# A linear-attention and token-mixing kernel: one load for w_phi, plain loads for the last weight rows, and kv blocks moved by matmuls

## The chip, the cores and the metric

One core of one Trainium2 chip. The metric is the device time of one execution in microseconds (us); smaller is better. The engines are TensorE (PE in the profile, with its weight loads as PEld), VectorE (DVE), ScalarE (ACT), GpSimd (POOL) and SyncE (SP). SP and ACT also issue the DMA transfers; each of the two has a DMA queue, and both queues run on the same 16 DMA engines. SBUF is the on-chip memory of 128 partitions, PSUM the accumulators that TensorE writes.

## The reference

`x` is 2048 tokens of 448 values, all in bf16. `xn` is its layer norm. Two branches read `xn`, and the output is `x + A(xn) + B(xn)`.

```python
# A: linear attention, 16 heads of 28
q, k, v = heads(xn @ wqkv)
pq, pk  = q @ w_phi[h], k @ w_phi[h]                    # a 28x28 matrix for each head
phi_q   = concat(softmax(pq), softmax(-pq))             # 56 features
phi_k   = concat(softmax(pk), softmax(-pk))
kv, z   = phi_k.T @ v, sum over tokens of phi_k
A       = concat_heads((phi_q @ kv) / (phi_q @ z + 1e-6)) @ wo
# B: a mixer
h  = gelu(layernorm(xn) @ w1)
hs = concat(h0 by +1 token, h1 by -1, h2 by +2, h3 by -2) @ w2
x1 = xn + hs
B  = x1 + gelu(layernorm(x1) @ w3) @ w4
```

## The kernel before

The tokens lie in 16 tiles of 128. Everything stays in SBUF between the steps; only `x`, the weights and the output cross to the chip's memory.

**Head.** `x` is loaded on SP's queue (tiles 0, 1, 2-3, then three transfers of four tiles). `wk` and `wq`, the key and query columns of `wqkv`, are loaded on ACT's queue and `wv` on SP's. The 448 rows of such a weight do not fill four blocks of 128 partitions, so `load_dup` (line 460) loads rows 0 to 383 in one transfer and then rows 384 to 447 *twice*, into both halves of the fourth block, by one transfer whose source reads the same 64 rows two times. TensorE transposes `wk` and `wq` (`trw`, line 653), and `fold` (line 674) multiplies them with `bd`, a matrix with the 28x28 blocks of `w_phi` on its diagonal, so that `xn @ wpk` gives `pk` at once. `bd` is zeroed by VectorE and filled by four DMAs on ACT's queue (line 503). VectorE and GpSimd make the layer norm: statistics and the scaling on VectorE, the power -1/2 on GpSimd (`ln_pow`, line 574). The first four tiles of `xn` are transposed by TensorE, the other twelve by DMA transposes on SP.

**K, V, Q.** For each pair of tiles, TensorE makes V (14 matmuls of 448 columns), K (14) and half of a Q group (14 of 512); ScalarE takes the exponentials of K and Q out of PSUM, ScalarE or VectorE copies V; VectorE sums the exponentials and GpSimd normalises (`phik<-phik,ksum`). W1 (`w,xnT`) follows, and after its last exponential ScalarE loads the gelu table (`warm2`, line 773) and takes the gelus of W1 (`gel`, `hq<-ps,fs`), which SP transposes one tile at a time by DMA into `hT`.

**The kv step.** 4 times 32 matmuls (`kv0` to `kv3`) sum `phi_k.T @ [v, 1]` over all tokens in one PSUM bank, two heads side by side in each of 8 column blocks. `kvc` (line 809) copies the bank to `kvs`. The wanted 28-row blocks stand on the partitions of `phi_k`; the numerator needs them on others, in `kvq`, with zeros around. Eight DMAs from SBUF to SBUF move them (line 819), seven of them issued by ACT and one by SP. `num` (line 888) waits for all of these.

**Mixer and end.** W2 (`w,hT`) reads `hT` of the tiles on both sides; VectorE adds `xn`, makes the second layer norm, and SP transposes it by DMA into `gT` (`gD`). H (`gT,w`) is the 448 to 1792 layer, followed by F (`w,phik` and `wo,xnT`), which sums both branches. Sixteen numerators (`kvq,eq`) are spread over this part.

Nothing here is in a hand-written order. The program is a list of tasks with a rank, dependencies and an assumed length; the class `Planner` (line 223) simulates the engines and fixes each engine's order, and for some tasks which of two engines takes them. `TI` and `TL` (line 448) are the assumed issue time and the assumed further delay of a DMA transpose. Each engine then runs its list strictly in order. `Recorder` derives the semaphore waits. All elementwise instructions are recorded from one line (L209), all activations from L205, all matmuls from L197, all plain DMAs from L212, the DMA transposes from L215. The names of tiles tell them apart; where memory is shared, a tile carries the name of its region (`wk`, `wq` and their transposes are `eq`, the gelu output and `wpq` are `hq`, the scaled `x1` is `wv`, numerator scratch is `vaug`, `h3` is `phik`, and attention outputs are `xnT`).

Of the kernel before, what the change touches and what calls it, by code (L numbers as in the profile page):

```python
# [5 lines left out]
ACT = mybir.ActivationFunctionType  # L6
ALU = mybir.AluOpType
# [338 lines left out]
def bass_parallel_sum__linear_kernel_hedgehog__mixer_s_mlp__prompt_kernel(  # L346
# [16 lines left out]
    with es:  # L363
# [53 lines left out]
        w4 = new("w4", FC * D).rearrange("p (c d) -> p c d", c=FC)  # L417
        gT = new("gT", 2 * 4 * 512).rearrange("p (b t c n) -> p b t c n", b=2, t=4, c=4)
        g_tok = view(wv_r, 4 * 512).rearrange("p (b t d) -> p b t d", b=2, t=2)
        kvs = new("kvs", 8 * 2 * HE).rearrange("p (c u n) -> p c u n", c=NC, u=2)  # L420
        kvq = new("kvq", 8 * 2 * HE).rearrange("p (c s n) -> p c s n", c=NC, s=2)
        ident = new("ident", 128)
        stat = {}
        for nm in ("st", "mv", "rs", "fs", "st2", "mv2", "rs2"):
            stat[nm] = new(nm, NT * 8, F32).rearrange("p (t c) -> p t c", t=NT)
        ksum = new("ksum", 8 * 32, F32).rearrange("p (b c) -> p b c", b=8)
        mhalf = new("mhalf", 8, F32)
        tiny = new("tiny", 2, F32)

        h3T = view(phik_r, 2 * FC * 512).rearrange("p (b c f) -> p b c f", b=2, c=FC)  # L430
# [14 lines left out]
        xs = carve(2 * D, F32).rearrange("p (b d) -> p b d", b=2)  # L445

        dve, pool = "DVE", "POOL"
        TI, TL = 1290, 1250
        P = Planner({"ps": 4, "h": 8, "g": 2, "gT": 2, "h3": 2, "o": 2, "oT": 2, "q": 2, "xs": 2, "ob": 4, "ks": 8})
        P.PATIENCE = {"PE": 60, "DVE": 80, "ACT": 80, "POOL": 80, "SP": 200}  # L450

# [7 lines left out]

        def load_dup(name, dst, src, rank, eng, cols=None, after=()):  # L460
            s = src if cols is None else src[:, cols]
            t = s[384:D, :]
            kb = 64 * (dst.ap[-1][1] * 2) / 1024
            twice = bass.AP(t.tensor, t.offset, [[0, 2]] + [list(a) for a in t.ap])
            return [load(name + "0", dst[:, 0:3, :], s[0:384, :].rearrange("(c p) d -> p c d", p=128), rank, eng, 6 * kb, after),
                    load(name + "1", dst[:, 3, :], twice, rank + 0.1, eng, 2 * kb, after)]

        def load(name, dst, src, rank, eng="SP", kb=100.0, after=()):
            return P.add(name, eng if isinstance(eng, dict) else {eng: 510}, None, rank, after,
# [28 lines left out]
        def memset(name, eng, ap, val, busy, rank):  # L498
            return P.add(name, eng, busy, rank, [], lambda t: R.ew(eng, "memset", ap, val))

        z_bd = memset("z_bd", dve, bd[0:CR, :], 0.0, 240, -20)
        phi4 = A_w_phi.rearrange("(c j) e f -> j e c f", j=4)
        l_bd = [P.add("bd%d" % j, "ACT", 690, -18.5 + j * 0.1, [z_bd],
                      lambda t, j=j: R.dma(bd[DH * j:DH * j + DH, :].rearrange("p (c f) -> p c f", c=NC)
                                           [:, :, DH * j:DH * j + DH], phi4[j], "ACT"), lag=1900) for j in range(4)]
        more_x(4, 4, -16)
        more_x(8, 4, -15)
        more_x(12, 4, -13)
# [7 lines left out]
                 [ident], [ident])  # L516

        t_id = P.add("ident", pool, 550, -19, [], ident_emit)
        t_mh = memset("mhalf", pool, mhalf[:, :], -0.5, 60, -18)
        z_h2 = memset("z_h2", pool, h_tok[:, 4:8, :, CR:128], 0.0, 330, 30)  # L520
        z_hT = memset("z_hTa", pool, hT[:, :, HALO - 2:HALO], 0.0, 60, 30)
# [127 lines left out]
        for t_, (w_sb, ld, rk) in enumerate(((wk, l_wk, -2), (wq, l_wq, -1))):  # L649
            nm = "kq"[t_]  # L650
            k = ("ps", "wT" + nm)

            def trw(t, w_sb=w_sb, k=k):
                for c in range(NC):
                    v = bank(P.slot[k], c // 2).bitcast(BF16)
                    for m in range(4):
                        R.tr(v[0:CR, 512 * (c % 2) + 128 * m:512 * (c % 2) + 128 * m + 128],
                             w_sb[:, m, CR * c:CR * c + CR], ident[:, :])
            tw = P.add("wT" + nm, "PE", 16 * (100 if t_ == 0 else 56), rk, ld + [t_id], trw, [k], mode=128)
            ev = []  # L660
            for d in range(2):
                def cp(t, k=k, d=d, t_=t_):
                    v = bank(P.slot[k], d).bitcast(BF16)[0:CR, :].rearrange("p (c n) -> p c n", c=2)
                    o = wT[0:CR, t_, 2 * d:2 * d + 2, :]
                    if t.eng == "ACT":
                        R.act(o, v, ACT.Copy)
                    else:
                        R.ew(dve, "tensor_copy", o, v)
                ev.append(P.add("wTc%s%d" % (nm, d), {"ACT": 905, "DVE": 620}, None, rk, [tw], cp, [k], lag=120))
            fold_done[nm] = []  # L670
            for mp in range(2):
                k2 = ("ps", "fold%s%d" % (nm, mp))

                def fold(t, k2=k2, mp=mp, t_=t_):
                    for d in range(2):
                        m = 2 * mp + d
                        for c in range(NC):
                            R.mm(bank(P.slot[k2], d)[:, CR * c:CR * c + CR], wT[0:CR, t_, c, 128 * m:128 * m + 128],
                                 bd[0:CR, CR * c:CR * c + CR], True, True)
                tf = P.add("fold%s%d" % (nm, mp), "PE", 8 * 49, rk + 2 + 5 * t_ + mp, ev + l_bd, fold, [k2], mode=128)  # L680

                def cpf(t, k2=k2, mp=mp, t_=t_):
                    v = both(P.slot[k2])[:, :, 0:D]
                    if t_ == 0:
                        o = wpk[:, 2 * mp:2 * mp + 2, :]
                    else:
                        o = wpq[:, 2 * mp:2 * mp + 2, :, :].rearrange("p b c (u d) -> p b (c u) d", u=2)[:, :, :, 0:56]
                        v = v.rearrange("p b (n d) -> p b n d", d=56)
                    if t.eng == "ACT":
                        R.act(o, v, ACT.Copy)  # L690
                    else:
                        R.ew(dve, "tensor_copy", o, v)
                fold_done[nm].append(P.add("foldc%s%d" % (nm, mp), {"ACT": 800, "DVE": 1010}, None, rk + 2 + 5 * t_ + mp,
                                           [tf] + ([z_wpq] if t_ else []), cpf, [k2]))
# [25 lines left out]
        for j in range(8):  # L720
# [15 lines left out]
            for i in (i0, i1):  # L736
                def red(t, i=i):
                    R.ew(dve, "tensor_reduce", ksum[:, P.slot[("ks", i)], :],
                         phik[:, i, 0:2 * D].rearrange("p (h e) -> p h e", e=DH), axis=AX.X, op=ALU.add)
                r1 = P.add("red%d" % i, dve, 1000, rk, ex, red, [("ks", i)], lag=110)  # L740

                def rec(t, i=i):
                    b = P.slot[("ks", i)]
                    R.ew(dve, "reciprocal", ksum[:, b, :], ksum[:, b, :])
                r2 = P.add("rec%d" % i, dve, 270, rk - 1, [r1], rec, [("ks", i)], lag=100)

                def nrm(t, i=i):
                    ph = phik[:, i, 0:2 * D].rearrange("p (h e) -> p h e", e=DH)
                    R.ew(t.eng, "tensor_tensor", ph, ph,
                         ksum[:, P.slot[("ks", i)], :].unsqueeze(2).to_broadcast([128, 2 * H, DH]), op=ALU.mult)  # L750
                k_ready[i] = P.add("nrm%d" % i, {"POOL": 1660, "DVE": 1000} if i in NRM_DVE else {"POOL": 1660}, None, rk, [r2], nrm, [("ks", i)])

        q_ready = {}
        for n in range(8):
# [52 lines left out]
                               + kv_pe[-1:], kv, [KV], mode=128))  # L807

        def kvc(t):
            R.ew(dve, "tensor_copy", kvs.rearrange("p c u n -> p (c u n)"), bank(P.slot[KV], 0)[:, 0:16 * HE])  # L810
        t_kvs = P.add("kvc", dve, 580, 100, [kv_pe[-1]], kvc, [KV])
        kv_dma = []
        for r in range(2):
            for s in range(2):
                for u in range(2):
                    def mvb(t, r=r, s=s, u=u):
                        p0, q0 = 56 * r + 28 * s, 64 * u + 28 * r
                        R.dma(kvq[q0:q0 + 28, :, s, HE * r:HE * r + DH + 1], kvs[p0:p0 + 28, :, u, HE * r:HE * r + DH + 1], t.eng)
                    kv_dma.append(P.add("kvd%d%d%d" % (r, s, u), {"SP": 850, "ACT": 560}, None, 125, [t_kvs, z_kvq], mvb, lag=2200))


        x1_ready, g_ready = {}, {}
# [3 lines left out]
        for j in range(8):  # L826
# [43 lines left out]
            def gd(t, j=j):  # L870
                R.dmaT(gT[:, P.slot[("gT", j // 2)], 2 * (j % 2):2 * (j % 2) + 2, :, :].rearrange("p t c n -> p (t c) n"),
                       g_tok[:, P.slot[("g", j)], :, :].rearrange("p t d -> p (t d)"))
            g_ready[i0] = g_ready[i1] = P.add("gD%d" % j, "SP", TI, G_RANK[j], ga, gd, gk, lag=TL)

        l_w3 = load_w("w3", w3, B_w3, 90, "SP", after=[xT_ready[15]])
        l_wo = load_dup("wo", wo, A_wo, 92, "SP", None, [xT_ready[15]])
# [6 lines left out]
        for i in range(NT):  # L883
# [4 lines left out]
            def num(t, i=i, g=g, jj=jj, k=k):  # L888
                bx, by = bank(P.slot[k], 0), bank(P.slot[k], 1)
                for s in range(2):  # L890
                    for c in range(NC):
                        at_ = 240 * s + 60 * c
                        for u, b in ((0, bx), (1, by)):
                            p = slice(64 * u, 64 * u + 56)
                            R.mm(b[:, at_:at_ + 60], eq[p, g, c, s, 128 * jj:128 * jj + 128], kvq[p, c, s, :], True, True)
            tn = P.add("num%d" % i, "PE", 8 * 28.5, NUM_RANK[i], q_ready[g] + kv_dma, num, [k] + ring, mode=64)

            def part(k, s):
# [51 lines left out]
            def od(t, i=i, g=g):  # L950
                R.dmaT(oT[:, P.slot[("oT", g)], i % 4 - 1:i % 4 + 1, :, :].rearrange("p t c n -> p (t c) n"),
                       o_tok[:, P.slot[("o", i // 2)], :, :].rearrange("p t d -> p (t d)"))
            oT_ready[i - 1] = oT_ready[i] = [P.add("oD%d" % (i // 2), "SP", TI, rk, [du], od, ok, lag=TL)]


        h3_ready = {}
# [97 lines left out]
```

## Time and profile before

| | us |
|---|---|
| median of 3 runs | 194.18 (193.66 to 195.72) |
| the profiled execution | 195.62 |
| its span in the profile | 193.7 |
| PE busy | 173.8 (90%) |
| DVE busy | 113.5 (59%) |
| ACT busy | 80.2 (41%) |
| POOL busy | 80.2 (41%) |

The profiled execution is 1.9 us longer than its span and 1.4 us above the median. Busy time on its own does not tell what an engine waits for: VectorE's 59% is an average over a stretch in which it is full and others in which it idles. A clock below 1.00 in the windows means that TensorE ran slower there. In the chain of waits, `ACTq` is ACT's instruction queue issuing a DMA, and `DMA` the time until a transfer's completion is seen.

### The profile page before, as it was taken

Reading aid. Unit: us, or ns where it says so; the run is one execution under the profiler, and the core shown is the slowest. Engines: PE = TensorE matmul, PEld = TensorE weight load, DVE = VectorE, ACT = ScalarE, POOL = GpSimd, SP = SyncE. Lnnn points to the kernel's source line nnn. Section 1 sums busy time; section 2 is a strip of 40 time slices with the busy share of each in tenths; the row PEclk is TensorE's granted clock in tenths of the full one; section 3 lists DMA queues with packets and bytes.
Section 4 is the critical chain, followed back from the end, with each engine's and each line's share of the span. In section 5 each row is a group of like instructions: output and inputs, shape, how many; then the busy total and the mean of one; then the engine's idle time right before and its main releaser. Section 6 shows DMA issues by size and latency. Waiting matters only on the chain.

```text
span 193.7 us, 4832 instructions
## 1 busy us (share of the span) xinstructions
PE 173.8 (90%) x2062; PEld 110.9 (57%) x2062; DVE 113.5 (59%) x298; ACT 80.2 (41%) x97; POOL 80.2 (41%) x121
## 2 busy tenths in 40 slices
PE   0228999999999959958999999999999999999994
PEld 0217555577666524424555666666666666666693
DVE  3614999978493255996999544292461677120222
ACT  0226889999997044203345213252042455200000
POOL 4501788999962010611343462052340642240440
PEclk9999999999999996997999999999999999999999
DMA  6984054669902626567109516027120122210111
GB/s 172 275 254 118 31 97 99 81 156 390 302 20 54 89 46 123 58 128 143 33 0 109 111 48 57 3 67 143 51 54 3 47 58 54 58 47 3 47 54 47
DMA packets 43864, 18.07 MB, mean 93 GB/s; under 512 B 34690, under 2 KB 43330, under 8 KB 43842
## 3 DMA queue, kind: packets, MB, share of 16 engines
q1 hardware_dynamic: 41108, 16.65, 38.5%
q10 hardware_dynamic: 2734, 1.10, 2.2%
q8 instruction: 16, 0.26, 0.6%
q14 instruction: 6, 0.05, 0.1%
HBM read 8.00 MB, written 1.84 MB: 51 GB/s over the span
## 4 chain that ended last, share of the span: by engine, by line
PE 82%; DMA 6%; DVE 4%; ACTq 4%; issue 1%; ACT 0%; DVEq 0%
PE ps L197 81%; DMA eq<-in_A_wqkv_dram 6%; ACTq L212 4%; PE ps L201 2%; DVE wv L209 1%; DVE xn L209 1%; DVE st L209 1%; DVE vaug L209 1%; ACT hq L205 0%; DVE kvs L209 0%; DVEq L169 0%; DVE mv L209 0%; DVE rs L209 0%
## 5 line engine op out<-in xcount | busy, mean ns | idle before, releaser
L205 ACT ACTIVATE phik<-ps 128x1024 bf16<-128x1024 f32 (+1 forms) x44 | 42.0, 1013 | 55.0 <-PE ps L197 55.0
L209 DVE TENSOR_TENSOR vaug<-ps,vaug 128x464 f32<-128x464 f32 (+3 forms) x66 | 32.5, 504 | 39.7 <-PE ps L197 38.4
L197 PE MATMUL ps<-gT,w 64*128 64x512 bf16 x392 | 48.4, 382 | 2.6 <-DVE st L209 2.0
L197 PE MATMUL ps<-w,phik 64*128 64x448 bf16 (+1 forms) x504 | 46.0, 328 | 0.0
L197 PEld LDWEIGHTS ps<-w,phik 64*128 64x128 bf16 x504 | 30.5, 94 | 12.5 <-DVE vaug L209 0.3
L197 PEld LDWEIGHTS ps<-gT,w 64*128 64x128 bf16 x392 | 23.4, 95 | 18.8 <-DVE st L209 2.4
L209 POOL TENSOR_TENSOR rs<-rs,mhalf 128x2 f32<-128x2 f32 (+1 forms) x17 | 11.4, 674 | 47.1 <-DVE rs L209 47.0
L209 POOL TENSOR_TENSOR vaug<-xn,xtok 128x448 f32<-128x448 bf16 x16 | 16.2, 1033 | 30.9 <-DVE vaug L209 30.9
L209 POOL TENSOR_TENSOR xnT<-vaug 128x224 bf16<-128x224 f32 x32 | 17.4, 566 | 24.5 <-DVE vaug L209 24.5
L209 POOL TENSOR_TENSOR phik<-phik,ksum 128x896 bf16<-128x896 bf16 x14 | 23.3, 1694 | 1.5 <-DVE ksum L209 1.5
L205 ACT ACTIVATE eq<-ps 120x1024 bf16<-120x1024 f32 (+1 forms) x19 | 19.3, 1100 | 5.9 <-PE ps L201 4.9
L209 DVE TENSOR_REDUCE ksum<-phik 128x32 f32<-128x896 bf16 x16 | 16.4, 1057 | 4.2 <-ACT phik L205 4.2
L197 PE MATMUL ps<-w,hT 48*128 48x448 bf16 (+1 forms) x128 | 17.6, 386 | 0.1
L197 PE MATMUL ps<-w,xnT 64*128 64x448 bf16 x112 | 14.2, 363 | 2.0 <-ACT hq L205 1.9
L201 PE MATMUL ps<-ident,eq 128*112 128x128 bf16 x32 | 4.4, 317 | 12.3 <-DMA eq<-in_A_wqkv_dram 12.2
L197 PE MATMUL ps<-xnT,hq 64*120 64x512 bf16 x112 | 15.0, 377 | 0.0
L205 ACT ACTIVATE hq<-ps,fs 128x448 bf16<-128x448 f32 x16 | 8.9, 634 | 12.9 <-DVE rs L209 7.5
L197 PE MATMUL ps<-wo,xnT 64*128 64x448 bf16 (+1 forms) x126 | 14.1, 328 | 0.0
L197 PE MATMUL ps<-wv,xnT 64*128 64x448 bf16 x112 | 13.5, 350 | 0.1
L209 DVE TENSOR_TENSOR xn<-ps,xn 128x896 bf16<-128x896 f32 x8 | 8.7, 1082 | 8.3 <-PE ps L197 8.3
L197 PE MATMUL ps<-wpk,xnT 64*128 64x448 bf16 x112 | 13.3, 349 | 0.0
L197 PEld LDWEIGHTS ps<-w,hT 48*128 48x128 bf16 (+1 forms) x128 | 7.7, 102 | 7.1 <-issue 1.6
(54 smaller groups left out, 159.4 us busy)
## 6 DMA issues: line engine op xcount, KB each, us to landing
w<-in_B_w_dram SPq DMA_DIRECT2D x2, 896.0 KB, 6.0
w<-in_B_w_dram SPq DMA_DIRECT2D x1, 1568.0 KB, 12.7
out_dram<-vaug SPq DMA_DIRECT2D x14, 112.0 KB, 1.7
xtok<-in_A_x_dram SPq DMA_DIRECT2D x3, 448.0 KB, 11.4
eq<-in_A_wqkv_dram ACTq DMA_DIRECT2D x2, 336.0 KB, 5.6
w<-in_B_w_dram SPq DMA_DIRECT2D x1, 392.0 KB, 8.6
wv<-in_A_wqkv_dram SPq DMA_DIRECT2D x1, 336.0 KB, 6.9
w<-in_B_w_dram SPq DMA_DIRECT2D x1, 336.0 KB, 9.3
```

The costliest lines, as they stand in the source:

```text
L197: self.op("PE", lambda e: e.matmul(out, lhsT, rhs, start=start, stop=stop, skip_group_check=True), [out], [lhsT, rhs], after=after)
L201: self.op("PE", lambda e: e.transpose(out, in_, ident), [out], [in_, ident])
L205: self.op("ACT", lambda e: e.activation(out, in_, func, **kw), [out], [in_] + aps)
L209: self.op(eng, lambda e: getattr(e, name)(out, *args, **kw), [out], aps)
L212: self.op(eng, lambda e: e.dma_start(out, in_), [out], [in_], dma=True)
```

## The change

Four parts, and two constants.

1. `load_dup` loads rows 384 to 447 by two plain transfers of 64 rows, one for each half of the fourth block, in place of one transfer that reads them twice. This holds for `wk`, `wq` (ACT's queue), `wv`, `w1`, `wo` (SP's).
2. `w_phi` is loaded by one transfer, first on ACT's queue, into `wphi` (112 partitions, one row of 28 values for each of 4 head groups). GpSimd makes `bd` from it by two block selections, each over 112 x 448, which keep the diagonal blocks and write zeros elsewhere. VectorE's zeroing of `bd` and four DMAs go. `bd`'s columns are stored in another order, and `fold` reads them with a stride.
3. `kvc` multiplies the kv bank with a 0/1 mask (`mask2`, made by GpSimd) while it copies, so that `kvs` holds zeros where the other head's values stood. Four matmuls (`kvm`) with a selection matrix (`pick`, copied from the identity by GpSimd) move the rows to their partitions in the second bank of the same PSUM slot, and two copies (`kvo`, each on VectorE or ScalarE) write `kvq`. The eight DMAs go.
4. The planner's assumed numbers: `TI` 1290 to 1310, `TL` 1250 to 1300, and a new `TL2` of 2000 for the transposes of `gT` and `oT`; VectorE's assumed length for a normalisation goes from 1000 to 1400.

```diff
-        TI, TL = 1290, 1250
+        TI, TL, TL2 = 1310, 1300, 2000
...
         def load_dup(name, dst, src, rank, eng, cols=None, after=()):
             s = src if cols is None else src[:, cols]
-            t = s[384:D, :]
             kb = 64 * (dst.ap[-1][1] * 2) / 1024
-            twice = bass.AP(t.tensor, t.offset, [[0, 2]] + [list(a) for a in t.ap])
-            return [load(name + "0", dst[:, 0:3, :], s[0:384, :].rearrange("(c p) d -> p c d", p=128), rank, eng, 6 * kb, after),
-                    load(name + "1", dst[:, 3, :], twice, rank + 0.1, eng, 2 * kb, after)]
+            three = load(name + "0", dst[:, 0:3, :], s[0:384, :].rearrange("(c p) d -> p c d", p=128), rank, eng, 6 * kb, after)
+            return [three] + [load(name + str(u + 1), dst[64 * u:64 * u + 64, 3, :], s[384:D, :], rank + 0.1 + 0.1 * u, eng, kb, after)
+                              for u in range(2)]
...
-        z_bd = memset("z_bd", dve, bd[0:CR, :], 0.0, 240, -20)
-        phi4 = A_w_phi.rearrange("(c j) e f -> j e c f", j=4)
-        l_bd = [P.add("bd%d" % j, "ACT", 690, -18.5 + j * 0.1, [z_bd],
-                      lambda t, j=j: R.dma(bd[DH * j:DH * j + DH, :].rearrange("p (c f) -> p c f", c=NC)
-                                           [:, :, DH * j:DH * j + DH], phi4[j], "ACT"), lag=1900) for j in range(4)]
+        l_phi = load("phi", wphi[0:CR, :, :], A_w_phi.rearrange("(c j) e f -> (j e) c f", j=4), -21, "ACT", 25)
+
+        def diag_emit(t):
+            full = wphi[0:CR, :, :].rearrange("p c f -> p (c f)").unsqueeze(1).to_broadcast([CR, 4, CR])
+            o = bd[0:CR, :].rearrange("p (j n) -> p j n", j=4)
+            R.op(pool, lambda e: e.affine_select(o, full, pattern=[[-DH, 4], [0, CR]], compare_op=ALU.is_ge,
+                                                 fill=0.0, base=0, channel_multiplier=1), [o], [full])
+            R.op(pool, lambda e: e.affine_select(o, o, pattern=[[DH, 4], [0, CR]], compare_op=ALU.is_ge,
+                                                 fill=0.0, base=DH - 1, channel_multiplier=-1), [o], [o])
+        l_bd = [P.add("bd", pool, 1400, -19, [l_phi], diag_emit)]
...
+        t_mask = P.add("mask", pool, 400, 50, [], mask_emit)
...
+        def pick_emit(t):
+            R.ew(pool, "tensor_copy", pick[0:CR, :, :].rearrange("p s (r e) -> p s r e", r=2),
+                 ident[0:CR, 0:CR].rearrange("p (r s e) -> p s r e", r=2, s=2))
...
         def kvc(t):
-            R.ew(dve, "tensor_copy", kvs.rearrange("p c u n -> p (c u n)"), bank(P.slot[KV], 0)[:, 0:16 * HE])
-        t_kvs = P.add("kvc", dve, 580, 100, [kv_pe[-1]], kvc, [KV])
-        kv_dma = []
-        for r in range(2):
+            R.ew(dve, "tensor_tensor", kvs[0:CR, :, :].rearrange("p c (r n) -> p c r n", r=2),
+                 bank(P.slot[KV], 0)[0:CR, 0:16 * HE].rearrange("p (c r n) -> p c r n", c=8, r=2),
+                 mask2[0:CR, :].unsqueeze(1).unsqueeze(3).to_broadcast([CR, 8, 2, HE]), op=ALU.mult)
+        t_kvs = P.add("kvc", dve, 580, 100, [kv_pe[-1], t_mask], kvc, [KV])
+
+        def kvm(t):
+            b = bank(P.slot[KV], 1)
             for s in range(2):
                 for u in range(2):
-                    def mvb(t, r=r, s=s, u=u):
-                        p0, q0 = 56 * r + 28 * s, 64 * u + 28 * r
-                        R.dma(kvq[q0:q0 + 28, :, s, HE * r:HE * r + DH + 1], kvs[p0:p0 + 28, :, u, HE * r:HE * r + DH + 1], t.eng)
-                    kv_dma.append(P.add("kvd%d%d%d" % (r, s, u), {"SP": 850, "ACT": 560}, None, 125, [t_kvs, z_kvq], mvb, lag=2200))
+                    R.mm(b[64 * u:64 * u + 56, 8 * HE * s:8 * HE * s + 8 * HE], pick[0:CR, s, :],
+                         kvs[0:CR, :, :].rearrange("p (c u) n -> p u c n", u=2)[:, u, :, :], True, True)
+        t_kvm = P.add("kvm", "PE", 4 * 103, 100, [t_kvs, t_pick], kvm, [KV], mode=128)
+        kv_dma = []
+        for u in range(2):
+            def kvo(t, u=u):
...
+            kv_dma.append(P.add("kvo%d" % u, {"DVE": 550, "ACT": 450}, None, 100, [t_kvm, z_kvq], kvo, [KV]))
...
-            g_ready[i0] = g_ready[i1] = P.add("gD%d" % j, "SP", TI, G_RANK[j], ga, gd, gk, lag=TL)
+            g_ready[i0] = g_ready[i1] = P.add("gD%d" % j, "SP", TI, G_RANK[j], ga, gd, gk, lag=TL2)
...
-            oT_ready[i - 1] = oT_ready[i] = [P.add("oD%d" % (i // 2), "SP", TI, rk, [du], od, ok, lag=TL)]
+            oT_ready[i - 1] = oT_ready[i] = [P.add("oD%d" % (i // 2), "SP", TI, rk, [du], od, ok, lag=TL2)]
```

Since the planner sees other tasks and other lengths, it also puts out other orders. In the schedule of the changed kernel the eight TensorE transposes of tiles 2 and 3 stand ahead of the first `fold`; ScalarE copies five V blocks in place of seven and VectorE three in place of one; W2 of the first pair follows `kv3` at once, with the four `kvm` matmuls between its two halves; H begins after W2 of four pairs of tiles, not five.

## The prediction

> **What bounds the kernel now.** I read the page's slices first, then the chain of waits, then windows around each hole.
>
> The slices: TensorE is full from about 20 us to the end, and what it lacks is a head of 15 us and some dents near 70 to 90 us, where its clock drops too.
>
> ```profile
> PE   0228999999999959958999999999999999999994
> ...
> PEclk9999999999999996997999999999999999999999
> ```
>
> The chain names the two places. In the head it waits 12.16 us for one weight transfer; later it runs through a copy of kv, seven DMA issues on ACT and a gelu before TensorE goes on.
>
> ```profile
> 2.84 12.16 DMA eq<-in_A_wqkv_dram
> ...
> 63.57 0.67 DVE kvs L209
> ...
> 64.26 0.96 ACTq L212
> ...
> 69.58 0.83 ACTq L212
> ...
> 71.00 0.64 ACT hq L205
> ...
> 92.03 98.89 PE ps L197 x1227
> ```
>
> Windows tell why. Read the last two columns (DMA share, GB/s) of the first two lines and TensorE's busy time and PEclk of the others.
>
> ```profile
> 6.00:8.00 2.00, 0.00 (x0) 0.00 (x0) 1.83 (x7) 0.00 (x0) 1.74 (x7) 1.00 1.01 324
> ...
> 16.00:17.00 1.00, 1.00 (x12) 1.00 (x11) 0.00 (x0) 1.00 (x2) 0.00 (x0) 1.00 0.14 47
> ...
> 69.40:71.68 2.28, 0.36 (x2) 0.10 (x3) 1.09 (x5) 1.22 (x3) 0.69 (x1) 1.00 0.11 10
> 71.68:76.20 4.52, 4.52 (x33) 2.02 (x34) 2.17 (x4) 3.13 (x6) 0.00 (x0) 0.62 0.58 114
> 82.50:84.85 2.35, 0.37 (x4) 0.03 (x1) 2.35 (x6) 0.00 (x0) 0.14 (x1) 1.00 0.85 167
> 86.90:90.00 3.10, 3.10 (x20) 1.66 (x18) 2.14 (x8) 1.02 (x1) 1.10 (x2) 0.55 0.79 156
> 92.03:190.92 98.89, 98.87 (x1250) 66.00 (x1250) 49.51 (x139) 26.96 (x30) 33.52 (x49) 1.00 0.27 52
> ```
>
> At 6 us all DMA engines work; from 15 us the share is 0.14, two engines of 16. The two holes at 69 and 82 us cost 1.9 and 2.0 us of idle time, and each is followed by a slow clock: (1 - 0.62) x 4.52 = 1.7 us and (1 - 0.55) x 3.10 = 1.4 us more. After 92 us TensorE is dense, so what is gained earlier should be kept.
>
> [...] seven issues of 6.3 KB hold ACT for 6.16 us, and gelus stand behind them.
>
> **Part 1, the last weight rows.** A doubled transfer puts 64 rows x 896 B = 57.3 KB on each of two engines, the main one 24 rows = 21.5 KB on each of 16. On those two, ACT's queue holds 157.6 KB up to the end of wq. If it gets half an engine and starts at 1.8 us, the landing at 15.05 us means 23.8 GB/s per engine. The same rate puts the other three at 3.6, 8.4 and 10.2 us; the matmuls that wait for them start at 4.4, 8.5 and 10.2. So this account stands, as an estimate. With plain loads (64 rows, 16 engines, 4 rows each) it is 57.3 KB on every engine: 1.8 + 2 x 57.3/23.8 = 6.6 us. ACT's queue has seven issues in the head, not eight; the last, at about 0.5 us each, is out by 4.2 us. For w_phi's small pieces ahead of it I add 1.4. wq lands at about 8, its 13 transposes (1.64 us) end by 10: 5 to 7 us earlier. SP's queue gets two more issues in the head (wv, w1, some 0.5 us each) and one for wo later; they hide, since SP's own transfers were limited by the same two engines (the third load of four x tiles took 10.4 us to land).
>
> **Part 2, w_phi.** Removed: 0.24 us of VectorE's zeroing (idle then) and four issues that held ACT until 8.5 us. Added: one load of 112 rows first on ACT's queue (+0.5 us before wk), and on GpSimd two selections of 448 columns. The selection of 128 columns took 0.29 us; by width that is 1.0, by the 896-wide multiply (1.69 us) 0.85. I take 0.9 each; bounds 0.3 and 2.0. They stand ahead of the first layer-norm power, which waits behind them. If w_phi lands at 3.7 (wk took 3.5 from issue), the power of tile 0 starts at 5.5, as before (5.44). Then GpSimd does hT's zeros, the mask (a fill, two tiny selections, 0.1 to 0.2 each), pick (0.25) and 0.93 for fs, 1.9 in all, before the powers of tile 1 (0.56) and 2-3 (0.69): 9.3 us. VectorE scales three tiles and copies (1.9), TensorE transposes (0.6), and fold starts at 11.9. That chain, not wq, is late next. Fold was at 17.33: 5.4 us earlier. Each us on it counts in full.
>
> After that ScalarE is full (9.9 of each 10 us from 30 to 60). It has two V copies fewer (2.0 us); VectorE, full from 20 to 40 us, has two more (2.1 us). But Q cannot start before ScalarE has copied wT, wpk, two K exponentials and wpq, which I follow to about 19.8 us, 5.3 ahead of before at equal work. I take **5.0 us** for the head, range 3 to 6.5.
>
> **Part 3, kv.** The masked copy costs what the plain one did (0.66). Four matmuls of 240 columns: the 224-wide ones take 0.26, overlapped, so 0.4 to 0.6 in all with the change of tiling. The copies are 464 wide: like the gelus (0.63) on ScalarE, 0.66 on VectorE. New waits: the matmuls stand on TensorE behind the first half of W2, which waits for hT of tiles 0 to 2. On ScalarE the copy stands behind six gelus and ahead of ten; if the matmuls are late those wait, and with them SP's transposes. From the first gelu G: a transpose is issued every 1.46 us and lands 2.6 us later, so W2 starts at G + 6.5 in both kernels (58.28 to 64.80 before). TensorE now arrives there 1.3 us early, since 14 W1 matmuls have moved behind. The matmuls end at G + 7.7, the copy at G + 8.5, and the seventh gelu starts at about G + 9.3 instead of G + 12.2. Its hT then comes in time for W2 of the third pair, so the first hole goes: 1.9 idle + 1.7 clock - 1.0 for the early arrival = **2.6**.
>
> H waits for gT of two pairs. I follow W2, the add (1.09), statistics (1.15), power (0.69), scaling (0.73) and transpose (3.3) to G + 20.7, where TensorE arrives too, with W2 of one pair (1.5 us) not yet done. Before it was G + 26.6. That is 4.4 us at equal work, the first hole among them, so the second hole gives 1.8; it may leave 0 to 3.5. Added matmuls: -0.4. Sum for the middle **4.0**, range 0 to 7. SP loses one kv issue (0.99), which hides.
>
> **Part 4.** Only orders change; the numbers above are for the new order. A new hole after 92 us would cost its width plus a slow clock, up to 3; I take 0.
>
> **Sum.** 5.0 + 4.0 = 9.0 us off the profiled execution: 195.62 (span 193.7 and 1.92 around it) becomes 186.6, span 184.7. The median is 1.44 below that execution, so the forecast for it is 194.18 - 9.0 = **185.2**.
>
> **Rivals.**
> - *Only the head pays* (chance 0.16). The kv matmuls, behind W2 on TensorE and ahead of gelus on ScalarE, open a new hole, with its slow clock. For it: W2 and the transposes have no slack at G + 6.5. Against: ACT's 6.16 us go. 194.2 - 5.0 = 189.2.
> - *Only the middle pays* (0.12). GpSimd's queue or VectorE, full at 20 to 40 us, replaces the transfer; the head gives 1. For it: the power chain above has no slack. Against: its rows add to 11.9 us. 194.2 - 1 - 4 = 189.2.
> - *Slower* (0.05). w_phi lands late in 56-byte pieces, and GpSimd, in order, holds all layer-norm powers behind its selections. Fold comes 8.2 us after that landing, so the head's gain is gone at 9.1 us, the middle's too at 13.1, and at 16 us the kernel ends at 197. For it: one w_phi issue was held 3.4 us before. Against: now nothing is ahead of it.
> - *The doubled read does not run on two engines*, or wq's wait has another cause: then wq stays late and only the middle pays, included above.
>
> **Chances and range.** The forecast's case has 0.67, with its own range 182 to 188. Head and middle at their best give 13.5, or 180.7; at worst the rivals of one part, with a stall of about 1, give 190.5. The range 181 to 190.5 leaves out the slower case and the tails. Differences under 1% are what a measurement here can hardly tell from none: faster 0.91, within it 0.04, slower 0.05.
>
> **What would show it.** In the changed profile: no stretch of DMA share near 0.14 before the transposes of wq, which end by 10 us; fold at 11 to 13; selections under 1 us each; no kv DMAs, first gelu near 53 us and the seventh some 9 us after it; clock 1.00 around 65 to 85. Wrong it would be by a landing of w_phi after 6 us, selections over 1.5 us, or a hole of over 2 us before a W2 or H group.

## The result

The changed kernel takes 186.64 us (median of four runs, 184.98 to 188.74) against 194.34 (193.66 to 195.72) for the kernel before: ratio 0.9567, 95% interval 0.9464 to 0.967. A second group of runs (e10 below) gives 186.03 against 194.01, ratio 0.9574 (0.9538 to 0.961). Medians here are over all executions, while ratios leave out those more than 1.5% above the fastest of the same kernel. The profiled execution took 184.98 us, with a span of 183.3.

The slices of the changed kernel, tenths of a slice. TensorE is full from about 10 us but for a dent at 69 to 78 us, and no slice has a lower clock:

```profile
PE   0499999999999997799999999999999999999993
...
PEclk9999999999999999999999999999999999999999
```

Its chain of waits (start, length, what). The weight transfer in the head is 5.50 us where it was 12.16; no ACT queue stands in the middle, but two DMA transposes do; the dense end starts at 91.92 us, as late as before (92.03), with 10.3 us less work left:

```profile
4.19 5.50 DMA eq<-in_A_wqkv_dram
...
9.82 2.79 PE ps L201 x29
...
57.97 3.96 DMA hT<-hq
...
69.45 4.54 DMA gT<-wv
...
91.92 88.57 PE ps L197 x1102
```

In the last full microsecond before wq lands all DMA engines work; the stretch on two engines is gone (last two columns: DMA share and GB/s):

```profile
8.00:9.00 1.00, 1.00 (x12) 1.00 (x11) 0.69 (x2) 0.00 (x0) 0.91 (x3) 1.00 1.10 315
```

For a table by stage I cut the trace at 28 us (all kernels are in the K and Q groups there) and at 97 us (all are dense). Each line is a window: its length, TensorE's busy time, then the other engines; the last columns are the granted clock, the DMA share and GB/s. Before:

```profile
0.00:28.00 28.00, 15.69 (x158) 10.89 (x160) 16.34 (x63) 12.82 (x15) 12.47 (x39) 1.00 0.58 161
28.00:97.00 69.00, 64.24 (x722) 36.84 (x720) 51.83 (x111) 41.97 (x55) 35.91 (x37) 0.95 0.54 122
```

After:

```profile
0.00:28.00 28.00, 20.50 (x212) 13.23 (x214) 22.93 (x81) 18.34 (x22) 20.73 (x56) 1.00 0.71 185
28.00:97.00 69.00, 66.07 (x786) 39.40 (x782) 56.20 (x121) 41.74 (x54) 34.99 (x34) 1.00 0.54 118
```

TensorE's idle time is 28 - 15.69 = 12.3 us in the head before and 7.5 after; in the middle 69 - 64.24 = 4.8 before and 2.9 after. So 4.8 + 1.8 = 6.6 us of the 10.4 us between the two spans are idle time. The rest is busy time (173.8 to 170.0 us), and most of that is the clock: the mean granted clock of the two profiled executions was 0.982 and 0.998, which over the spans is 3.5 and 0.4 us.

The same cut through the traces of the experiments, with the median of each kernel, its ratio to the kernel before on the same chip, and the mean time of those of its executions whose mean clock was at least 0.998 ("full clock", with their number):

| kernel | head idle | middle idle | median us | ratio (95%) | full clock |
|---|---|---|---|---|---|
| before (e11's profile) | 12.2 | 4.2 | 194.15 | 1.001 (0.998 to 1.004) | 193.5 (37) |
| e1: 128 rows instead of 64 twice | 5.7 | 4.7 | 186.78 | 0.963 (0.958 to 0.968) | 186.4 (2) |
| e2: the change, loads on two engines | 14.6 | 2.9 | 194.10 | 1.000 (0.997 to 1.003) | 193.8 (15) |
| e7: kv part alone | 12.5 | 3.3 | 193.53 | 0.988 (0.981 to 0.995) | 191.3 (1) |
| e9: plain loads alone | 6.1 | 3.5 | 186.03 | 0.957 (0.952 to 0.962) | 186.0 (4) |
| e12: loads and kv part | 6.1 | 2.3 | 184.87 | 0.951 (0.945 to 0.957) | 184.6 (3) |
| e5: the same, with the new constants | 6.4 | 3.0 | 184.88 | 0.950 (0.943 to 0.956) | 184.5 (4) |
| the change (e10) | 7.7 | 2.8 | 186.03 | 0.957 (0.954 to 0.961) | 186.05 (7) |
| e14: the change, w_phi last | 6.5 | 3.7 | 186.21 | 0.957 (0.950 to 0.964) | 185.5 (2) |
| e3: the change, kv by DMAs | 8.4 | 4.5 | 188.33 | 0.971 (0.965 to 0.977) | 187.5 (2) |

The full-clock mean of before is over 37 of the 71 executions of it whose clock I have; that of the change takes in both groups of runs. A difference of 1 to 2 us in this table rests on few executions: those of the change alone go from 184.98 to 187.43 us at full clock. The profile of e7 is one at a mean clock of 0.982, that of e14 one at 0.991.

### The profile page after: what moved, and what is told of

It reads as the page before. It is cut to its first block, busy times and chain, and to the rows that moved or that the text cites. A ratio compares the mean times of both kernels' runs of the same rounds, so it can differ in the third digit from the quotient of the medians.

```text
span 183.3 us, 4828 instructions
## 1 busy us (share of the span) xinstructions
PE 170.0 (93%) x2066; PEld 109.6 (60%) x2066; DVE 115.6 (63%) x300; ACT 80.1 (44%) x96; POOL 82.9 (45%) x127
## 3 DMA queue, kind: packets, MB, share of 16 engines
q10 hardware_dynamic: 1872, 1.06, 2.2%
## 4 chain that ended last, share of the span: by engine, by line
PE 85%; DMA 8%; ACT 3%; ACTq 2%; DVE 1%; issue 0%; DVEq 0%
PE ps L197 83%; DMA eq<-in_A_wqkv_dram 3%; DMA gT<-wv 2%; DMA hT<-hq 2%; ACTq L212 2%; PE ps L201 2%; ACT phik L205 1%; ACT hq L205 1%; DVE xn L209 1%; DVE wv L209 0%; DVE vaug L209 0%; DVEq L169 0%; DVE st L209 0%
## 5 line engine op out<-in xcount | busy, mean ns | idle before, releaser
L205 ACT ACTIVATE phik<-ps 128x1024 bf16<-128x1024 f32 (+1 forms) x44 | 42.8, 1025 | 55.7 <-PE ps L197 55.6
L197 PE MATMUL ps<-gT,w 64*128 64x512 bf16 x392 | 47.4, 376 | 2.0 <-DMA gT<-wv 1.9
L209 POOL TENSOR_TENSOR phik<-phik,ksum 128x896 bf16<-128x896 bf16 x14 | 24.0, 1745 | 3.2 <-DVE ksum L209 3.2
L197 PE MATMUL ps<-w,hT 64*128 64x448 bf16 (+1 forms) x128 | 15.7, 350 | 0.8 <-ACT phik L205 0.4
L197 PEld LDWEIGHTS ps<-w,hT 48*128 48x128 bf16 (+1 forms) x128 | 7.1, 94 | 6.6 <-ACT phik L205 1.0
L197 PEld LDWEIGHTS ps<-xnT,hq 64*120 64x120 bf16 x112 | 8.0, 130 | 4.4 <-PE ps L197 0.5
```

Source lines behind the costliest of these rows:

```text
L197: self.op("PE", lambda e: e.matmul(out, lhsT, rhs, start=start, stop=stop, skip_group_check=True), [out], [lhsT, rhs], after=after)
L205: self.op("ACT", lambda e: e.activation(out, in_, func, **kw), [out], [in_] + aps)
L209: self.op(eng, lambda e: getattr(e, name)(out, *args, **kw), [out], aps)
```

## The experiments

**e1: does the doubled read cost because of its engines?** The kernel before, but the second transfer of each weight reads rows 320 to 447, 128 different rows, in place of rows 384 to 447 twice. Bytes, issues and orders stay; rows 320 to 383 then stand where copies of the last 64 should, so the products are others.

```diff
-            t = s[384:D, :]
...
-            twice = bass.AP(t.tensor, t.offset, [[0, 2]] + [list(a) for a in t.ap])
+            twice = s[320:D, :]
```

> The kernel before with one edit: the second transfer of wk, wq, wv, w1 and wo reads the 128 different rows 320 to 447 into the fourth block, not rows 384 to 447 twice. Bytes, number of transfers and the order on every engine stay as before; what is computed changes, since the upper half of the block holds other rows. Theory (the doubled read runs on two of 16 DMA engines, this one on 16): wq lands at 9 to 10 us and not at 15, no stretch with a DMA share near 0.14 before it, time 189.5 (188 to 191). Rival (what pays is fewer bytes or smaller pieces, or wq waits for something else): wq lands at about 15, time 194.

Measured: 186.78 us, 7.5 less than before and better than the 188 to 191 expected; the transposes of wq start at 8.39 and the fold at 10.66 us, and in the slice of its page from 4.6 to 9.2 us the DMA share is 0.9 or more, at 357 GB/s. One access pattern, and nothing else, holds nearly the whole gain. It is the pattern of all five weights at once; the chain names wq, and the others were not tried one by one. Its chain of waits:

```profile
2.26 6.08 DMA eq<-in_A_wqkv_dram
```

**e2: the same cause put back into the change.** The two loads of 64 rows are written as 2 x 32 rows whose steps overlap, so that their slowest dimension is 2. Of the 64 rows each then reads one twice and leaves the last one out, so the last 32 rows of weights are shifted by one.

```diff
+            t = s[384:D, :]
+            two = bass.AP(t.tensor, t.offset, [[31 * t.ap[0][0], 2], [t.ap[0][0], 32], list(t.ap[1])])
-... dst[64 * u:64 * u + 64, 3, :], s[384:D, :], ...
+... dst[64 * u:64 * u + 64, 3, :], two, ...
```

> The changed kernel with one edit: each plain transfer of 64 rows is written as 2 x 32 rows with a step of 31, so that the slowest dimension of its source is 2; no row but one is read twice, row 447 is left out (the result changes by that). The order on every engine is that of the changed kernel. Theory (the number of engines decides): the two DMA engines hold as much as before, wq lands at about 15 to 16 us with a DMA share of 0.13 ahead of it, time 191.5 (190 to 193). Rival (reading the same rows twice is what was slow): wq lands at 9.7 as in the changed kernel, time 186.6.

Measured: 194.1 us, ratio 0.9997 (0.9967 to 1.0028), above the 190 to 193 expected. The transposes of wq start at 17.11 us, and ahead of them the windows show the signature of before, a DMA share that falls to 2/16 at 47 GB/s with TensorE idle:

```profile
15.00:16.00 1.00, 0.00 (x0) 0.00 (x0) 0.00 (x0) 0.00 (x0) 0.00 (x0) 1.00 0.17 56
16.00:17.00 1.00, 0.00 (x0) 0.00 (x0) 0.63 (x1) 0.00 (x0) 0.00 (x0) 1.00 0.13 47
```

So the repeated reading, which is down to a single row here, is not the cause, and the number of transfers isn't either. What the two slow kernels share is a slowest dimension of 2, with a share of 0.14 (before) and 0.13 (e2); with 128 rows (e1) it is 0.9 or more, with 64 (the change) 1.10. Other sizes were not run. With this undone, the rest of the change nets nothing that can be measured. That sum has two sides: the middle has 1.3 to 1.9 us less idle time than before, and the head 2.3 to 2.4 us more.

**e9 and e7: the parts alone.** e9 is the kernel before with part 1 only; e7 is it with part 3 only.

```diff
 e9: load_dup as in the change; w_phi, kv step and constants as before
 e7: kvc, kvm, kvo, mask2 and pick as in the change; loads, w_phi and constants as before
```

> The kernel before with the plain 64-row loads alone. The planner orders the head anew. Theory (the spread over 16 engines is the whole of the head's gain, as the 128-row kernel showed): 187 (186 to 188.5), wq landing at 9 to 10. Rival (the extra issue on the queue per weight and the other order give part of it back): 189 to 191.

> The kernel before with the kv part alone (mask, selection, four matmuls, two copies in place of eight DMAs); loads, w_phi and constants as before. The planner orders the middle anew. Theory of the forecast (the part takes away both holes and their slow clock): 190.3. Rival, after the undone kv part has cost the changed kernel little: the slow clock behind the holes is not there in every execution, and the part is worth 1 to 2.5: 192.5. Second rival: nothing, 194.3.

Measured: the loads alone give 186.03 us, all that the whole change gives on the same chip. The kv part alone gives 193.53, ratio 0.988. Two of its four executions had a mean clock of 0.982, so its gain is only bracketed: 0.5 us between the medians, 2.2 at full clock (one execution). In e7 the first hole is gone (only 0.35 us of waiting for `hT`), but a hole of 2.65 us in front of H has taken its place:

```profile
67.33 0.74 PE L197 MATMUL ps<-w,hT 48*128 48x448 bf16 x5 [0.35 <-DMA hT<-hq]
...
82.55 3.41 PE L197 MATMUL ps<-gT,w 64*128 64x512 bf16 x14 [2.65 <-DMA gT<-wv]
```

The middle's idle time falls by 0.9 to 1.5 us, not by the two holes.

**e3: the kv part taken out of the change.** The eight DMAs are back, with `kvs` and `kvq` laid out as before.

```diff
...
-            R.ew(dve, "tensor_tensor", kvs... mask2..., op=ALU.mult)
-        t_kvm = ...; kvo0, kvo1 = ...
+            R.ew(dve, "tensor_copy", kvs..., bank(P.slot[KV], 0)[:, 0:16 * HE])
+                        R.dma(kvq[q0:q0 + 28, :, s, ...], kvs[p0:p0 + 28, :, u, ...], t.eng)
```

> The changed kernel with the kv part undone: plain copy to kvs, eight DMAs, no matmuls, mask and selection unused. The planner orders the middle anew. Theory (seven issues hold ACT ahead of gelus and open a hole on TensorE with a slow clock behind it): about 6 us of issues between gelus, a hole of 1 to 2 us, time 190 (188.5 to 191.5). Rival (only the head pays, the kv part is worth nothing): 186.6 (within 1).

Measured: 188.33 us. ScalarE's timeline shows the six issues that the planner gave to ACT, and the gelus behind them:

```profile
53.79 1.14 ACT L205 ACTIVATE hq<-ps,fs 128x448 bf16<-128x448 f32 x2
...
61.10 5.81 ACTq L212 DMA_DIRECT2D kvq<-kvs  x6
66.96 2.21 ACT L205 ACTIVATE hq<-ps,fs 128x448 bf16<-128x448 f32 x4 [7.16 <-PE ps L197]
```

The seventh gelu is at G + 13.2 us (G is the first gelu) where the change has it at G + 9.2, yet the kernel loses only 1.4 us at full clock (187.5 in two executions against 186.05), or 2.3 between the medians; the middle has 1.5 to 1.7 us more idle time, and the head, in another order, 0.7 to 0.9. So most of this hold of ACT does not reach the end. What absorbs it was not tried; TensorE has W1 matmuls and numerators between the gelus.

**e8: a hold of ACT by itself.** The change, with ten copies of `wphi` onto itself on ACT behind its kv copy.

```diff
+                if t.eng == "ACT":
+                    for _ in range(10):
+                        R.act(wphi[0:CR, :, :], wphi[0:CR, :, :], ACT.Copy)
```

> The changed kernel with ScalarE held: right after its kv copy ten copies of wphi onto itself, about 0.6 us each, 6 us in all, ahead of the last ten gelus. Orders otherwise unchanged. Theory (holding ScalarE there is what the DMAs cost): later hT, a hole before W2 of the second or third pair, time 190.5 (189 to 192). Rival (ScalarE has slack there and the DMA's landing was the cost): below 188.

Measured: the ten copies took 3.23 us, about half of what I had reckoned with, so the hold is smaller than planned and the expectation was not tested at its size. The seventh gelu is at G + 11.4, TensorE waits 2.1 us for `hT`, and the time is 187.87 us. That is 1.9 us at full clock (187.93 in four executions against 186.05) for a hold of 3.2. A hold of 5.81 us cost 1.4 to 2.3 in e3, where the kv matmuls, the copies and VectorE's share of them are gone as well. So the price of a hold lies between a quarter and 0.6 of its length, and isn't settled more closely than that.

**e5: the w_phi part taken out of the change.** Four DMAs on ACT's queue behind wq fill `bd` again.

```diff
-        l_phi = load("phi", wphi[0:CR, :, :], ..., -21, "ACT", 25)
...
-        l_bd = [P.add("bd", pool, 1400, -19, [l_phi], diag_emit)]
+        z_bd = memset("z_bd", dve, bd[0:CR, :], 0.0, 240, -20)
+        l_bd = [P.add("bd%d" % j, "ACT", 690, -18.5 + j * 0.1, [z_bd], ...) for j in range(4)]
```

> The changed kernel with the w_phi part undone: bd zeroed by VectorE and filled by four DMAs on ACT's queue behind wq, no selections on GpSimd. Theory (w_phi's load only has to come before fold, the part moves little): wq lands at 8.7 instead of 9.7, fold some 0.5 to 1 us earlier, time 186 (185 to 187.5). Rival (four issues hold ACT up to 8 us and bd lands late, so the part was worth something): fold waits for bd, 188 or more.

Measured: 184.88 us, faster than the change on the same chip (186.03); at full clock 184.5 against 186.0. All four executions of it (182.91 to 185.27) are shorter than all four of the change there (185.83 to 186.21). The head's idle time is 6.4 us, not 7.5 to 7.7. So the w_phi part is a loss, of 1.2 us between the medians and 1.5 at full clock.

**e10: the changed kernel again,** unchanged, on the chip of e5, e7 and e9.

> The changed kernel as it is, beside the other three on one chip. Expected 186.5 (185 to 188.5), wq landing at 9 to 11 us, seven gelus' distance between the first and the seventh about 9.2 us.

Measured: 186.03 us (185.83 to 186.21). The fold is at 13.20 us, the first gelu G at 53.14 and the seventh at G + 9.2.

**e14: is it the place of w_phi's load?** The change, with w_phi's load behind wk and wq on ACT's queue.

```diff
-... "(c j) e f -> (j e) c f", j=4), -21, "ACT", 25)
+... "(c j) e f -> (j e) c f", j=4), -18.5, "ACT", 25)
```

> The whole change, but w_phi's load stands behind wk and wq on ACT's queue. The change costs about 1.1 us more than e5, which has w_phi by four DMAs behind wq. If that is the place of the load ahead of wk and wq (one issue of about 0.5 us and its small pieces ahead of both weights): wk's and wq's transposes start 0.6 to 1 us earlier than in the change (5.7 and 9.8 us), the fold near 12, and the time is about 185, near e5. If it is the two selections on GpSimd ahead of layer-norm powers: they still stand ahead of the power of tiles 2 and 3, fold stays at 12.5 or later, and the time is 186 to 187, as the change.

Measured: 186.21 us. The later transposes of wk start at 6.04 us (at 7.49 in the change), and the head's idle time is 6.5, near e5. But w_phi landed only at 11.7, the selections fell ahead of the power of tiles 2 and 3 in GpSimd's order, and their third line here is that power, waiting behind them (it starts at 12.94; in e5 at 9.01):

```profile
11.73 0.59 POOL L508 TENSOR_SCALAR_AFFINE_SELECT bd<-wphi 112x448 bf16<-112x448 bf16 x1 [3.77 <-DMA wphi<-in_A_w_phi_dram]
12.39 0.58 POOL L510 TENSOR_SCALAR_AFFINE_SELECT bd<-bd 112x448 bf16<-112x448 bf16 x1
12.94 0.70 POOL L209 TENSOR_TENSOR rs<-rs,mhalf 128x2 f32<-128x2 f32 x1
```

The head's loss is mostly gone, but two things moved at once: the load's place in the queue, and on GpSimd the selections, which now stand behind the powers of tiles 0 and 1 (5.71 us, as in e5). So e14 doesn't tell one from the other. The time doesn't follow either (the middle has 0.7 to 0.9 us more idle time), and the intervals of e14, e5 and the change overlap.

**e12: the constants.** e5 with the planner's constants of before.

```diff
-        TI, TL, TL2 = 1310, 1300, 2000
+        TI, TL, TL2 = 1290, 1250, 1250
-... {"POOL": 1700, "DVE": 1400} ...
+... {"POOL": 1660, "DVE": 1000} ...
```

> The loads and the kv part, with w_phi by four DMAs as in e5_phi_dma and the planner's constants as before the change. The constants change only orders. If they are worth nothing, as forecast: the time of e5, 184.9 us (183.5 to 186). If they are what brings e5 below e9_loads_alone (186.0): 186 to 187.

Measured: 184.87 us, e5's time. The constants are worth nothing that shows, beside the loads and the kv part. These two kernels are the fastest of the study.

**e13: less traffic beside wq.** e5, with SP's later loads held until VectorE has the statistics of tile 2.

```diff
+            if i == 4:
+                return P.add("x4", "SP", 510, rank, [], lambda t: R.op(
+                    "SP", lambda e: e.dma_start(o, s), [o], [s, stat["st"][:, 2, 0:6]], dma=True), ...)
...
+                    for late in [lx[4], lx[8], lx[12]] + l_w1 + l_w2:
+                        late.deps.append(s)
```

> e5_phi_dma, with SP's loads of x tiles 4 to 15, w1 and w2 held until VectorE has the statistics of tile 2 (about 6 us); they are about 2 MB that share the 16 DMA engines with wk and wq. The forecast's account of the head has wq landing at the rate of half of the DMA engines. If that sharing now sets wq's landing (the DMA share is 1.1 at 8 to 10 us): wq lands 1.5 to 2 us earlier, at about 8, and the time is near 183.5. If the chain of layer norm, transposes and fold has become as late, as forecast ("that chain, not wq, is late next"): wq's transposes move earlier, fold by less than 0.7, and the time stays at 184.5 to 185.5. If the later x tiles come too late for the V and K groups: a new hole of 1 us or more near 20 us, and 186 or more.

Measured: 186.85 us (183.95 to 188.74). Held until 6.29 us, the loads moved neither wq's transposes nor the fold (9.91 and 13.09 in e5):

```profile
9.90 1.64 PE L201 MATMUL ps<-ident,eq 128*112 128x128 bf16 x13 [0.36 <-DMA eq<-in_A_wqkv_dram]
...
13.08 1.21 PE L197 MATMUL ps<-bd,eq 112*128 112x112 bf16 x11
```

From 3 to 13 us the DMA share is 1.01 or more in each microsecond with the hold, and without it too, but for one of 0.90 (5 to 6 us in e5). So this hold did not free the engines when wq needed them. Two of the four executions had a mean clock of 0.982 (188.4 us) and the others 183.95 and 185.62, so nothing about the time follows.

**e11: the kernel before, once more.** No edit. It asks whether the slow clock behind the two holes, which the forecast counted, comes every time.

> The kernel before, unchanged, for a second profile of it. The forecast counted a slow clock behind each of the two holes, 1.7 and 1.4 us, as a cost that the kernel pays every time. If so: TensorE's clock in the profile is near 0.98 again, and near 0.88 in the stretch from the kv copy to the dense end. If the slow clock only comes in some executions, as e1 (the order of before, the same two holes, clock 1.00) suggests: the holes of about 2 us are there again, the clock is 1.00 in all or in one of them, and the profiled execution is 1.5 to 3 us shorter than the 195.6 us of the first.

Measured: 194.15 us, the profiled execution 194.23 with a mean clock of 0.991. In its windows the first hole (1.0 us of idle time, with 0.57 more at 66 us) leaves the clock at 1.00, and the second (1.4 us) is followed by 0.69 and 0.82 (the last two lines). In the first profile 1.9 and 2.0 us were followed by 0.62 and 0.55; in e1, with the order of before, holes of 1.26 and 0.83 us, in the change one of 1.85 and in e3 one of 2.3 left it at 1.00:

```profile
70.00:72.40 2.40, 1.38 (x14) 0.42 (x9) 1.56 (x6) 1.22 (x3) 0.69 (x1) 1.00 0.12 11
72.40:76.00 3.60, 3.60 (x51) 2.03 (x53) 2.43 (x5) 3.19 (x6) 0.00 (x0) 1.00 0.44 90
77.00:79.80 2.80, 1.36 (x27) 0.67 (x23) 2.80 (x6) 1.16 (x2) 2.05 (x3) 1.00 0.82 89
79.80:83.30 3.50, 3.48 (x21) 1.49 (x21) 2.78 (x8) 0.00 (x0) 1.35 (x2) 0.69 0.62 120
83.30:86.80 3.50, 3.39 (x26) 1.60 (x28) 3.50 (x10) 0.11 (x1) 0.27 (x1) 0.82 0.65 130
```

The mean clocks of 71 executions of the kernel before fall into steps: 37 at 0.998 or more (mean 193.5 us), 30 at 0.991 (194.8), 4 at 0.982 (195.7). The step of 0.009 is 1.7 us of a span of 193, and a slow stretch costs as much: in the first profile each of the two loses 1.7 us by the clock, with 0.50 in its middle (73 to 76 and 87 to 89 us), and e11's two lines with 0.69 and 0.82 lose 1.7 us together. At 0.50 that is some 3.4 us. By the times a step is 1.3 us, less than the lost clock. The execution profiled at the start, 195.62 us, was one of the rare ones with two.

## Why the prediction was right, and where it was off

The total was right: 185.2 forecast, 186.6 and 186.0 measured, inside the range of 181 to 190.5 and clearly faster. The profiled execution was forecast at 186.6 and took 184.98. By parts it was not right: the loads alone gave 8.0 us where the forecast had 5.0 for them and w_phi together, the kv part gave 0.5 to 2.3 (by e7, e3, and e9 against e5 and e12) where it had 4.0, and the w_phi part lost 1.2 to 1.5. That these come near the forecast sum is in part luck. Step by step:

- **The two engines** are shown, from both sides: a DMA share of 0.14 before and 0.13 in e2, 1.10 in the change and 0.9 or more in e1. The loads of four tiles of `x` gain too: their median from issue to landing was 11.4 us and is 7.1. That plain loads of 64 rows would spread over all 16 engines was an estimate of mine; what the runs show is the share.
- **The head's 5.0 us** came out at 4.8 (idle time up to 28 us), but not by the path that I followed. "That chain, not wq, is late next" failed. In the chain of waits after the change, wq lands at 9.69 us, 29 transposes follow it without a gap, then the fold (12.45, forecast 11.9); no power of GpSimd is in it. wq is 1.7 us later than my 8, because the 57.3 KB per engine of ACT's queue (an estimate, its bytes over 16) took 7.9 us from 1.8 us on, 7.3 GB/s and not half of 23.8: all queues together moved 306 GB/s in that time, 19.1 per engine, and wk and wq got 0.38 of it. The chain through the powers was 1 us earlier than forecast (`xn` of tiles 2 and 3 is scaled at 10.2 us, not 11.2). Two sizes were off against each other, so that the fold came near its forecast is luck. The loads alone give 6.2 us in the head (e9, 12.3 to 6.1), and the w_phi part takes 1.2 to 1.4 of them back.
- **w_phi.** Landing (forecast 3.7, the selection starts at 3.26), selections (0.9 each, measured 0.59 and 0.58) and the power of tile 0 (5.5, measured 4.46) were all better than forecast, and the part still lost 1.2 to 1.5 us. The step that failed: I took its load ("+0.5 us before wk" and 1.4 us of pieces, an estimate without a measurement behind it; packets under 512 bytes run from 2.2 to 3.0 us, so about 0.8) and its selections as hidden, since something else would be late. The later transposes of wk do start at 7.49 us in the change and at 5.98 in e5, but that alone need cost nothing as long as TensorE waits for wq afterwards, and wq's last transposes start no later in the change (9.82, and 10.06 in e10) than in e5 (9.91) and e14 (10.09). What differs is the work that TensorE has before then: 19 transposes in the change, 27 in e5 and e14, with eight of `xn` among them. The change, then e5:

```profile
7.49 2.00 PE L201 MATMUL ps<-ident,eq 128*112 128x128 bf16 x16 [1.28 <-DMA eq<-in_A_wqkv_dram]
9.82 1.61 PE L201 MATMUL ps<-ident,eq 128*112 128x128 bf16 x13 [0.34 <-DMA eq<-in_A_wqkv_dram]
11.22 1.39 PE L201 MATMUL ps<-ident,xn 128*128 128x128 bf16 x16
...
5.98 1.64 PE L201 MATMUL ps<-ident,eq 128*112 128x128 bf16 x13 [0.96 <-DMA eq<-in_A_wqkv_dram]
7.41 1.06 PE L201 MATMUL ps<-ident,xn 128*128 128x128 bf16 x8
9.30 2.25 PE L201 MATMUL ps<-ident,eq 128*112 128x128 bf16 x16 [0.83 <-DMA eq<-in_A_wqkv_dram]
```

In the change tile 1 is scaled only at 8.92 us (6.84 in e5). On GpSimd its power waits behind the selections, the mask and `pick` (7.03; in e5 the powers of tiles 0 and 1 begin at 5.68), and on VectorE a copy of wk's transposes stands ahead of the scaling. Which of the two counts, the load's place or GpSimd's order, stays open.

- **The kv step's middle, 4.0 us.** Its mechanism is right in part: the seventh gelu comes at G + 9.2 (forecast 9.3), and the first hole shrank from 1.9 to 0.3 us. But the gelus' delay weighed less than forecast, as e3 and e8 show. The terms without the clock (1.9 - 1.0 + 1.8 - 0.4 = 2.3, the last for added matmuls, of which the four of 240 columns took 0.39 us) stand against 1.8 us less idle time. By time at full clock the kv part is worth about 1.4: e3's loss of 1.4, and from e9 to e5 and e12 a gain of 1.5 and 1.4, each of few executions. The second hole stayed, 1.85 us at 74 us: H came at G + 22.1, not 20.7, since the transpose into `gT` that it waits for took 4.54 us where I had 3.3.
- **The term that was mis-sized is the clock,** "1.7 clock", together with "the median is 1.44 below that execution". I took one execution's slow clock as paid every time, and subtracted it in full from a median of executions of which, by e11's count, half had paid nothing. Over the 71 executions the mean loss to the clock is 1.0 us, over the eight of the change 0.3. So the clock gives about 0.7 between the kernels, not 1.7, and that 1.0 us is as large as the gap between the forecast and the second group of runs (185.2 and 186.0) and most of that to the first (1.4). The account isn't closed: idle time (6.6) and clock (0.7) make 7.3 us, while the medians differ by 7.7 and 8.0. Against the profiled execution alone, which had lost 3.5 us to the clock, the forecast was too small by 1.6 us: it left the second slow stretch out, 1.7 us by the clock of each microsecond from 86 to 90 us (0.64, 0.50, 0.50, 0.65).
- **The constants** at 0: shown (e12 against e5).
- **The rivals.** "Only the head pays" and "only the middle pays" both put 189.2. Part 1 alone gives 186.0 and part 3 alone 193.5: the parts don't fit that division, because the loads bring nearly the whole gain. The first also named a new hole at the kv matmuls, and there is none. "Slower" is ruled out by the time, and w_phi landed before 3.3 us.

## What to carry to other kernels

Look at the DMA share in the last stretch before a late transfer. Here a steady 2/16 (0.14, 47 GB/s) meant that an access pattern, not the bytes, set the landing: wq's last transposes started at 15.05 us, and at 8.39 with one transfer of 128 different rows (e1) or 9.82 with two of 64 (the change), which takes one more transfer. What was tried is a slowest dimension of 64 and of 128 in place of 2. Before a clock term read from one profile is subtracted from a median, count it in several executions, since the same hole can leave the clock alone or halve it (1.00 behind the first hole in e11's profile, 0.50 from 73 to 76 us in the first profile). And undo each part of a change that bundles several: here one part brought all the gain, one about 1.4 us, and one took about as much away. A transfer that lands earlier is worth only what the engine behind it can do with it: when TensorE still has to wait for a later one, the work that stands ahead of that wait decides (19 transposes in the change, 27 in e5).

## What the runs showed of the hardware

- The clock behind a hole is not a fixed price. The same program has a mean clock of 0.998 or more in 37 of 71 executions, 0.991 in 30 and 0.982 in 4, which by the 1.7 us of one slow stretch is none, one and two. Idle times of 1.85 us in the change and 2.3 in e3 left the clock at 1.00 where 1.4 us in e11 brought 0.69. TensorE does run at half speed in such a stretch: before, eight matmuls of W2 took 1.88 us from 74.50 us on, at 0.50, and 0.93 from 76.43 on, at 1.00. What decides whether a hole is followed by one was not shown.
- The same normalisation of 128 x 896 can take twice its time. In the change's trace VectorE took 2.56 us for one at 47.02 us, beside GpSimd's own, and 1.02 for one at 51.97; GpSimd took 2.41 for the one that began at 52.13, where the median of its fourteen is 1.69. Whether the two hold each other up was not tried.
- Holding back the later loads of `x` by 2.3 us, and those of `w1` and `w2` by 1.4 (e13), did not bring wq a tenth of a microsecond sooner; the DMA share stayed at 1.06 or more while they were held.
